# A fused attention and SwiGLU kernel: the RMSNorm of the first two batches taken out of the activations and put into the gate product, the output and the copies

## The chip, the cores and the metric

The kernel runs on one core of one Trainium2 chip. The metric is the device time of one execution in microseconds (us). Four executions of the kernel before gave 471.46 to 472.03 us, with a median of 471.5. The span of a profiled execution, from the first to the last instruction, is about 2 us shorter than its time (469.9 for 471.5).

In the profile, PE is the matmul engine (TensorE), DVE the vector engine, ACT the scalar engine (ScalarE), POOL the GpSimd engine. "L314" is a line of the kernel that was profiled. Line numbers move between kernels, so I compare groups by the names of their tiles.

## The reference

Eight batches, twelve heads, 448 tokens, head size 64. Attention has one more term in the denominator ("softmax off by one"). Its result becomes 3584 tokens of 768 features, which go through RMSNorm and a SwiGLU block (768 to 1536 to 768). Inputs and outputs are fp32; the kernel multiplies in bf16.

```python
scores = q @ k.T / sqrt(64)
m      = max(scores);  e = exp(scores - m)
x      = e / (sum(e) + exp(-m)) @ v          # -> 3584 x 768
xn     = x / sqrt(mean(x*x) + 1e-6) * rms_g  # RMSNorm, per token
g, val = xn @ w_gate, xn @ w_val             # 768 -> 1536
out    = (g * sigmoid(g) * val) @ w_out      # 1536 -> 768
```

Two facts of this algebra make the change possible. The factor 1/rms is one number per token, so it may be multiplied in after a product as well as before it. The factor rms_g is one number per feature, so it may sit in x or in the weights.

## The kernel before

PE follows one program order in which the feed-forward of a batch (24 "products" of 6 matmuls, gate and value in turn) is mixed with the attention of the next batch. DVE and ACT work in their own program orders: before 40.17 us of the trace DVE stood 1.68 us for a tanh. Batches 0 and 1 (`NPE = 2`) turn x on PE; the later batches turn it by DMA.

The normalization of x in batches 0 and 1, with 1/rms per token (`rinv`), then the turn of x on PE:

```python
def emit_scale(b, c):
    nc.vector.tensor_scalar(out=x_tiles[b][:, c, :], in0=x_tiles[b][:, c, :],
                            scalar1=xnt_tiles[b, "r"][:, c:c + 1], ...)
def emit_turn_x(b, c):
    if b < NPE:
        ps = ps_f.tile([128, KD, P], BF16, name="xnt_ps", tag="f")
        for dk in range(KD):
            nc.tensor.transpose(ps[:, dk, :], xn[:, c, dk * 128:(dk + 1) * 128], ...)
        # copied to xnt_sb by ACT or DVE
    else:
        nc.sync.dma_start_transpose(out=xnt[:, c, :, :], in_=xn[:, c, :])
```

A product and what follows it. `t_sb` is tanh(g/2), and (t_sb + 1) * g is twice g * sigmoid(g); the output's factor 0.5 takes the 2 back. I call the DVE instruction that makes `silu` the *second step*.

```python
def emit_A(b, m, part):
    ...
    for dk in range(KD):
        nc.tensor.matmul(ps[:, 0:S], lhsT=w[:, dk, m * 128:(m + 1) * 128], rhs=xnt_tiles[b][:, :, dk, :], ...)
    if part == 0:   # gate
        nc.scalar.activation(out=t, in_=ps[:, 0:S], func=AF.Tanh, scale=0.5)
        nc.vector.scalar_tensor_tensor(out=u, in0=t, scalar=1.0, in1=ps[:, 0:S], op0=ALU.add, op1=ALU.mult)
    else:           # value
        nc.vector.tensor_tensor(out=ht_tiles[...], in0=g_cur.pop((b, m)), in1=ps[:, 0:S], op=ALU.mult)
```

Between batch 0's attention and its feed-forward. `scale_w` multiplies rms_g into a piece of the weights; `warm` issues matmuls that only keep PE busy.

```python
emit_root(0)            # mean of squares, then POOL's power: rinv
scale_w(2, V); scale_w(1, A)
warm(14)
for c in range(C):
    emit_scale(0, c)
scale_w(1, V)
for c in range(C):
    emit_turn_x(0, c)
...                     # more scale_w
```

The softmax here doesn't subtract the row's maximum and nothing guards it: scores larger than these inputs give would overflow.

## Time and profile before

| | before |
|---|---|
| median of 4 executions | 471.5 us |
| profiled span, mean clock of PE | 469.9 us, 0.998 |
| PE busy | 456.2 us (97%) |
| DVE busy | 240.8 us (51%) |

The table of busy time in the profile page of the kernel before (share of the span, count of instructions):

```profile
PE 456.2 (97%) x4051; PEld 246.0 (52%) x4051; DVE 240.8 (51%) x621; ACT 249.4 (53%) x365; POOL 95.4 (20%) x109
```

The table of stretches of the kernel before. The rows are: the last attention of batch 0 to its first product, batch 0's feed-forward with batch 1's attention, batch 1's feed-forward with batch 2's attention, and the rest. The columns are the stretch and its length, the busy time and count of each engine, PE's granted clock, the DMA share and GB/s:

```profile
core 0: us, PE busy (x) PEld busy (x) DVE busy (x) ACT busy (x) POOL busy (x), PEclk, DMA share, GB/s
29.15:35.21 6.06, 5.23 (x56) 3.02 (x53) 4.99 (x19) 4.20 (x9) 1.15 (x1) 1.00 1.30 240
35.21:88.43 53.22, 48.46 (x533) 25.09 (x533) 39.34 (x94) 33.24 (x49) 23.67 (x27) 1.00 0.89 175
88.43:126.03 37.60, 37.60 (x343) 19.37 (x342) 21.78 (x53) 23.03 (x32) 9.40 (x9) 1.00 0.84 169
126.03:469.90 343.87, 339.48 (x2774) 184.20 (x2770) 156.50 (x402) 166.57 (x249) 43.71 (x42) 1.00 0.52 111
```

PE is full in batch 1's feed-forward (37.60 busy of 37.60 us). What can be won lies earlier. PE's timeline there (start, busy time, line, what was computed, and in brackets the idle time before it with what ended it):

```profile
29.03 3.19 PE L360 MATMUL warm_ps<-blank 128*128 128x512 bf16 x14
32.79 1.73 PE L280 MATMUL xnt_ps<-identity,x_sb 112*128 112x112 bf16 x24 [0.57 <-DVE x_sb L271]
...
35.21 1.30 PE L314 MATMUL g_ps<-xnt_sb,wg_bf 128*128 128x448 bf16 x6
```

The 3.19 us of warming matmuls are time in which PE has no real work, because x is still being normalized. This is the hole that the change aims at. PE's list of waits from 35 to 89 us (total, times, longest), its three largest, shows how little it waits for in batch 0's feed-forward:

```profile
PE g_ps L314 <- DVE ht_sb L325: 1.8, 1, 1.8
PE u_ps L240 <- DVE x_sb L244: 1.5, 3, 1.1
PE v_ps L314 <- DVE wv_bf L125: 0.7, 1, 0.7
```

### The profile page before, as it was taken

To read this page: it belongs to the slowest core of one execution; us is meant where nothing else is said; L and a number is where in the kernel's file an instruction comes from. 1 tells how busy PE (TensorE), PEld (TensorE's weight loads), DVE (VectorE), ACT (ScalarE), POOL (GpSimd) and SP (SyncE) were. 2 spreads that over 40 slices of the span, in tenths; PEclk is the share of its full clock that TensorE was granted. 3 is DMA by queue.
4 is the path that set the end of the run, shared out by engine and by line. 5 is a ranking of instruction groups with operands and counts; after the bars stand their busy time and mean duration, and the time that the engine had idled before them with its cause. 6 is when DMAs were issued, how large, how long until landed. Compare 5 with 4: busy or idle time off the path is not lost.

```text
span 469.9 us, 9847 instructions
## 1 busy us (share of the span) xinstructions
PE 456.2 (97%) x4051; PEld 246.0 (52%) x4051; DVE 240.8 (51%) x621; ACT 249.4 (53%) x365; POOL 95.4 (20%) x109
## 2 busy tenths in 40 slices
PE   8989997999999999999999999999999999999996
PEld 3554543554555555455465545545455555555563
DVE  4676698445632176645742265854743247555200
ACT  4987763655566565464546555555556652222221
POOL 7434454114012211322002211313000000000000
PEclk9999999999999999999999999999999999999999
DMA  8999974999079896495049988299015221100133
GB/s 130 223 224 200 212 178 101 213 220 207 1 157 206 214 203 146 85 214 115 0 108 202 227 188 161 45 183 174 14 36 126 69 68 22 38 1 0 36 100 102
DMA packets 86937, 60.48 MB, mean 129 GB/s; under 512 B 50678, under 2 KB 81980, under 8 KB 86892
## 3 DMA queue, kind: packets, MB, share of 16 engines
q1 hardware_dynamic: 73980, 43.60, 43.5%
q0 software_dynamic: 12912, 16.26, 18.7%
q8 instruction: 32, 0.52, 0.5%
q14 instruction: 13, 0.11, 0.1%
HBM read 47.19 MB, written 11.01 MB: 124 GB/s over the span
## 4 chain that ended last, share of the span: by engine, by line
PE 89%; DVE 4%; ACT 2%; DMA 1%; issue 1%; POOL 1%; ACTq 0%; POOLq 0%
PE o_ps L339 24%; PE v_ps L314 23%; PE g_ps L314 18%; PE u_ps L240 10%; PE s_ps L209 9%; PE s_ps L314 5%; DMA k_bf<-in_k_dram 1%; ACT p_sb_110 L214 1%; DVE x_sb L271 1%; PE qkt_ps L182 1%; DVE x_sb L244 1%; ACT p_sb_108 L214 1%; ACT t_sb L318 1%; DVE wv_bf L125 0%; DVE xsq L266 0%
## 5 line engine op out<-in xcount | busy, mean ns | idle before, releaser
L314 PE MATMUL v_ps<-xnt_sb,wv_bf 128*128 128x448 bf16 x576 | 125.1, 353 | 0.7 <-DVE wv_bf L125 0.7
L339 PE MATMUL o_ps<-wo_bf,ht_sb 128*128 128x384 bf16 x672 | 116.5, 326 | 0.0
L314 PE MATMUL g_ps<-xnt_sb,wg_bf 128*128 128x448 bf16 x444 | 96.4, 353 | 1.9 <-DVE ht_sb L325 1.8
L339 PEld LDWEIGHTS <-ht_sb 128*128 128x128 bf16 x672 | 62.6, 98 | 46.2 <-issue 7.8
L314 PEld LDWEIGHTS <-wg_bf 128*128 128x128 bf16 x576 | 52.2, 97 | 55.3 <-issue 12.3
L314 PEld LDWEIGHTS <-wv_bf 128*128 128x128 bf16 x576 | 52.4, 98 | 52.5 <-issue 8.2
L318 ACT ACTIVATE t_sb<-g_ps 128x448 f32<-128x448 f32 x74 | 40.3, 545 | 67.6 <-PE g_ps L314 67.6
L214 ACT ACTIVATE p_sb_108<-s_ps 112x896 bf16<-112x896 f32 x64 | 55.6, 915 | 14.9 <-PE s_ps L209 14.8
L214 ACT ACTIVATE p_sb_110<-s_ps 112x896 bf16<-112x896 f32 x64 | 55.9, 915 | 12.5 <-PE s_ps L209 12.5
L342 ACT ACTIVATE out_sb<-o_ps 128x384 f32<-128x384 f32 x56 | 27.5, 491 | 65.2 <-PE o_ps L339 55.8
L214 ACT ACTIVATE p_sb_109<-s_ps 112x896 bf16<-112x896 f32 x64 | 55.8, 918 | 10.2 <-PE s_ps L209 10.2
L243 DVE RECIPROCAL recip<-u_ps 112x4 f32<-112x4 f32 x96 | 17.1, 178 | 80.2 <-PE u_ps L240 80.1
L244 DVE TENSOR_TENSOR x_sb<-u_ps,recip 112x256 bf16<-112x256 f32 x96 | 40.7, 424 | 3.3
L158 POOL CAST q_bf<-q_f 112x1024 bf16<-112x1024 f32 x17 | 17.7, 1043 | 101.0 <-DMA q_f<-in_q_dram 75.7
L209 PE MATMUL s_ps<-qk_t 64*128 64x448 bf16 x272 | 37.5, 354 | 0.0
L297 POOL TENSOR_TENSOR rinv<-ms,neghalf 112x4 f32<-112x4 f32 x8 | 8.3, 1032 | 143.8 <-DVE ms L291 138.8
L266 DVE CUSTOM_DVE_ANT_0 xsq<-x_sb 112x256 bf16<-112x256 bf16 (+3 forms) x62 | 33.9, 547 | 1.6
L318 ACT ACTIVATE t_sb<-s_ps 128x448 f32<-128x448 f32 x22 | 12.0, 544 | 38.5 <-PE s_ps L314 33.3
L314 PE MATMUL s_ps<-xnt_sb,wg_bf 128*128 128x448 bf16 x132 | 28.6, 352 | 0.0
L240 PEld LDWEIGHTS <-p_sb_110 112*128 112x128 bf16 (+1 forms) x512 | 19.6, 97 | 7.8 <-DVE x_sb L244 1.4
L240 PEld LDWEIGHTS <-p_sb_109 112*128 112x128 bf16 (+1 forms) x512 | 19.9, 97 | 5.9 <-issue 1.2
L240 PEld LDWEIGHTS <-p_sb_108 112*128 112x128 bf16 (+1 forms) x512 | 19.3, 98 | 7.0 <-issue 2.7
(278 smaller groups left out, 382.7 us busy)
## 6 DMA issues: line engine op xcount, KB each, us to landing
q_f<-in_q_dram SPq DMA_DIRECT2D x15, 448.0 KB, 4.7
k_f<-in_k_dram SPq DMA_DIRECT2D x15, 448.0 KB, 6.0
v_f<-in_v_dram SPq DMA_DIRECT2D x15, 448.0 KB, 7.4
v_f<-in_v_dram POOLq DMA_DIRECT2D x9, 448.0 KB, 8.7
out_dram<-out_sb SPq DMA_DIRECT2D x7, 336.0 KB, 3.0
wg_bf<-in_moe_w_gate_dram POOLq DMA_DIRECT2D x2, 1152.0 KB, 16.3
wv_bf<-in_moe_w_val_dram POOLq DMA_DIRECT2D x2, 1152.0 KB, 14.5
wo_bf<-in_moe_w_out_dram POOLq DMA_DIRECT2D x3, 768.0 KB, 13.6
```

What stands on the lines that cost most here:

```text
L158: eng.tensor_copy(out=dst, in_=staged[n, i].rearrange("p h c d -> p c h d"))
L209: nc.tensor.matmul(s_ps[:, hh, 0:S], lhsT=k_t[r, k0:k0 + 128], rhs=qs[r], start=True, stop=True)
L214: nc.scalar.activation(out=p_v, in_=s_ps[0:P, :, 0:S], func=AF.Exp, scale=scale)
L240: nc.tensor.matmul(u_ps[:, qc, :], lhsT=p_sb[0:K, q0:q0 + 128], rhs=v_sb[0:K, c, h, :], start=(c == 0), stop=(c == C - 1))
L243: nc.vector.reciprocal(out=recip, in_=u_ps[0:P, :, D:E1])
L244: nc.vector.tensor_tensor(out=x_tiles[b][:, :, h * D:(h + 1) * D], in0=u_ps[0:P, :, 0:D], in1=recip.to_broadcast([P, C, D]), op=ALU.mult)
L266: nc.vector.tensor_tensor_reduce(out=xsq[:, 0:n], in0=x_c, in1=x_c, scale=1.0, scalar=0.0, op0=ALU.mult, op1=ALU.add, accum_out=acc)
L297: nc.gpsimd.tensor_tensor(out=rinv, in0=ms, in1=neghalf, op=ALU.pow)
L314: nc.tensor.matmul(ps[:, 0:S], lhsT=w[:, dk, m * 128:(m + 1) * 128], rhs=xnt_tiles[b][:, :, dk, :], start=(dk == 0), stop=(dk == KD - 1))
L318: nc.scalar.activation(out=t, in_=ps[:, 0:S], func=AF.Tanh, scale=0.5)
L339: nc.tensor.matmul(o_ps[:, 0:HN], lhsT=ht_tiles[b2][:, fk, c * 128:(c + 1) * 128], rhs=wo_bf[:, fk, n * HN:(n + 1) * HN], start=(fk == 0), ...
L342: nc.scalar.activation(out=o_sb[:, n * HN:(n + 1) * HN], in_=o_ps[:, 0:HN], func=AF.Copy, scale=0.5)
```

## The change

The intent: do not wait for 1/rms before the first products. x of batches 0 and 1 is turned raw, two heads (a "pair") at a time, as soon as attention has made it. rms_g goes into the copies of the turned pairs, so the weights need no scaling at first; the 24 scalings of the weights move to later, for batches 2 to 7. 1/rms is multiplied into the gate product (it must go in before tanh) and into the output, where it takes care of the value product. For the gate it is needed as a row along the free axis, the same on all partitions: a diagonal matrix is built by DVE and multiplied by ones on PE (the "spread"). For the output it is needed as 7 columns: eight tiny fp32 matmuls. The change also re-times what stands around it: batch 1's attention starts 3.5 units later in the schedule of batch 0's feed-forward (5.7 instead of 2.2, where a product is 1.13 units), and POOL's loads and casts move with it.

The core of the diff (cut at each "..."):

```diff
+    def emit_turn_pair(b, j, eng):
+        ps = ps_f.tile([128, C, P], BF16, name="xnt_ps", tag="f")
+        for c in range(C):
+            nc.tensor.transpose(ps[:, c, :], x_tiles[b][:, c, j * 128:(j + 1) * 128], ...)
+        # copied by ACT or DVE, times gain[:, j:j + 1]
+    def emit_diag(b):
+        nc.vector.tensor_tensor(out=diags[b]..., in0=identity..., in1=xnt_tiles[b, "r"]..., op=ALU.mult)
+    def emit_spread(b):
+        nc.tensor.matmul(ps, lhsT=ones, rhs=diags[b], start=True, stop=True)
+        nc.scalar.copy(out=rinv_b[b], in_=ps)
+    def emit_columns():
+        ...  # eight times
+                nc.tensor.matmul(ps[done:done + take, i:i + 1], lhsT=rinv_b[b][0:1, t:t + take],
+                                 rhs=ones[0:1, 0:1], start=True, stop=True)
+        nc.vector.tensor_scalar(out=rinv_c, in0=ps, scalar1=0.5, ...)
...
+                gate = ps[:, 0:S]
+                if b < NPE:
+                    gate = out_pool.tile(...)[:, 0:S]
+                    nc.vector.tensor_tensor(out=gate, in0=ps[:, 0:S], in1=rinv_b[b], op=ALU.mult)
+                nc.scalar.activation(out=t, in_=gate, func=AF.Tanh, scale=0.5)
+                nc.vector.scalar_tensor_tensor(out=u, in0=t, scalar=1.0, in1=gate, ...)
...
-                             func=AF.Copy, scale=0.5)
+                             scale=rinv_c[:, c:c + 1] if 2 * b2 < NPE else 0.5)
...
+    for j in range(NP):
+        ops.append((T1 + STEP * (j + 1) + 2.5 + (j == NP - 1), lambda j=j: emit_turn_pair(1, j, (A, V)[j % 2])))
+    for i in range(2 * KD):
+        ops.append((42.0 + 1.0 * i, lambda: scale_w(1, V)))
+        ops.append((55.0 + 1.9 * i, lambda: scale_w(1, V)))
...
     emit_AV(NP - 1, 1)
-    scale_w(1, A)
+    emit_A(0, 0, 0, 0, KD - 1, "s")      # three products, as far as pairs 0 to 4 go
+    emit_A(0, 0, 1, 0, KD - 1)
+    emit_turn_pair(0, NP - 1, A)
     emit_root(0)
-    scale_w(2, V)
-    warm(14)
-    ...                                  # emit_scale, emit_turn_x, scale_w
+    load_w(1)                            # a weight load issued by POOL
+    cast_qkv(NG, 2, G)                   # a cast by POOL
+    emit_A(0, 1, 0, 0, KD - 1, "s")
+    emit_A(0, 0, 0, KD - 1); emit_A(0, 0, 1, KD - 1); emit_A(0, 1, 0, KD - 1)
+    emit_diag(0)
+    emit_spread(0)
+    emit_A(0, 1, 1)
+    emit_T(NP)                           # q and k of batch 1's first pair turned
+    emit_A(0, 2, 0, bank="u")
```

## The prediction

> **What bounds the kernel.** TensorE (PE): busy 456.2 of 469.9 us (busy table), clock 0.998. The table of stretches shows no PE idle time from 88 to 420 us. What can be won lies earlier: the start of the feed-forward, and 4.7 us of PE idle from 51 to 82 us.
>
> **The aim.** PE's timeline from 29.0 to 35.2 us, between batch 0's last attention product and the first feed-forward matmul: 14 warming matmuls (3.2 us), 0.57 idle, 24 transposes of x (1.73), transposes of q/k (0.5). DVE's timeline shows why: squares, POOL's power, scalings, turn. Afterwards most of three products starts at once, on raw x.
>
> **Removed and moved.** Warm block, idle, turning of x: about 5.3 us of PE. In 51 to 82 us, 12 weight scalings on DVE (0.33 to 1.19 us each) and batch 1's scalings of x (three took 3.1 us); PE waited 0.74 us for a scaled weight and 1.76 + 0.36 us for DVE there (list of waits); these should go.
>
> **Added (estimates from the trace).**
> - The 1/rms chain now sits in PE's order. The pair's copy (0.5 us) stands before ScalarE's squares, then power 1.15, diagonal 0.6, [...]copy 0.5. PE should idle about 2 us before the spread, and 1.9 us more before batch 1's first q/k transposes, whose bank the first value product still holds. So most of the 5.3 us comes back: at 42 us at most 1 us ahead.
> - Pair copies in batch 0, where DVE is full: 0.45 us.
> - 24 gate multiplies on DVE, 0.54 us each like the other 448-column fp32 operations: 13 us. Worse, gate multiply, tanh and second step are consecutive on an in-order DVE. [...]the trace agrees (DVE idles 1.0 to 1.7 us for t_sb). So DVE stands 0.7 us per gate, and a gate/value pair holds it 2.3 us, where PE needs 2.27, or 3.15 with attention between.
> - Batch 1's feed-forward (88 to 126 us, PE full, DVE 22 of 38 us) gets 12 of these, plus 12 weight scalings (up to 1.2 us beside a POOL cast) in its second half. DVE then needs about 22 us where PE needs 17. Three banks and the next stage absorb perhaps 2 us; I expect 2 to 5 us of PE waiting.
> - [...]columns 0.5 us of PE.
>
> **Sum.** Start -0.5 (-3 to +1); batch 0's feed-forward -1.5 (-4 to +1); columns +0.5; batch 1's feed-forward +3 (0 to +6). From 150 us on nothing changes. That gives 473; as I may overstate DVE's standing, I predict **472.0 us, range 465.5 to 478.5**. Chances: faster by over 2% 0.03, within 2% 0.88, slower by over 2% 0.09.
>
> **What would show it.** PE timeline: no warm block at 29 us; 2 us idle before the fp32 spread; a second wait before batch 1's first q/k transposes. Without these the start gains 3 us. PE waits: scaled weights gone; new ones on DVE's products in batch 1's feed-forward. DVE timeline: gate multiply, gap of 0.7 us, second step; busy time up by 9 us.
>
> **What would make it wrong.** If free banks cover DVE's standing, PE stays full in batch 1's feed-forward and the result is 466 to 468. Value weights landing late (30.1 us before, just when needed) would add up to 1 us.

The sum came to -0.5 - 1.5 + 0.5 + 3 = +1.5 us on 471.5, which is the 473. The 0.5 us for the columns and the 2 us that banks absorb are estimates, without a trace behind them.

## The result, and the profile after

The changed kernel is correct and slower: a median of 490.95 us (four executions, 489.71 to 494.2) against 471.5. The ratio is 1.042, with a 95% interval of 1.037 to 1.0471. Ratios here are the mean time of one kernel's fast runs over that of the other's fast runs of the same rounds, so they are not quite the ratio of the medians that I quote. The profiled span grew from 469.9 to 488.9 us, by 19.0. This is far outside the predicted range.

Busy time in the profile page after, and the table of stretches. The rows are now: the first product to batch 1's first scores, just before the seventh product (46.28 us); to batch 1's first product; to the first output product; the rest. Two short stretches are put between:

```profile
PE 461.9 (94%) x4054; PEld 249.3 (51%) x4054; DVE 257.7 (53%) x649; ACT 248.8 (51%) x363; POOL 95.5 (20%) x109
```

```profile
core 0: us, PE busy (x) PEld busy (x) DVE busy (x) ACT busy (x) POOL busy (x), PEclk, DMA share, GB/s
30.59:46.28 15.69, 11.45 (x64) 5.19 (x61) 8.55 (x21) 3.01 (x8) 2.96 (x3) 0.78 1.19 218
37.00:38.00 1.00, 0.00 (x0) 0.00 (x0) 0.96 (x1) 0.00 (x0) 0.47 (x1) 0.50 1.15 209
46.28:98.93 52.65, 42.46 (x498) 22.92 (x499) 35.65 (x79) 31.88 (x47) 23.38 (x27) 1.00 0.78 163
98.93:144.16 45.23, 41.75 (x359) 21.72 (x357) 31.15 (x73) 21.13 (x30) 7.40 (x7) 0.96 0.51 107
127.00:129.00 2.00, 2.00 (x8) 0.59 (x5) 1.30 (x4) 1.48 (x3) 0.00 (x0) 0.50 0.00 0
144.16:488.90 344.74, 339.72 (x2768) 184.38 (x2767) 162.67 (x419) 169.79 (x251) 44.19 (x42) 1.00 0.52 110
```

PE is now idle for 10.2 us of batch 0's main stretch and for 3.5 us of batch 1's feed-forward, and its clock was halved twice, from 36.9 to 43.7 us and from 125.7 to 129.1. The starts of the products in the two timelines divide the 19.0 us:

| stretch | before | after | difference |
|---|---|---|---|
| up to the seventh product of batch 0 | 46.78 | 46.77 | 0.0, but see below |
| from there to batch 1's first product | 41.65 | 52.16 | +10.5 |
| from there to the first output product | 37.60 | 45.23 | +7.6 |
| from there to the end | 343.87 | 344.74 | +0.9 |

The first row is not as even as it looks. At its seventh product the kernel before had also done two turns of q and k, three groups of scores and two attention products of batch 1, which the changed kernel had not: 3.6 us of PE by the durations in the trace (0.5, 0.49 and 0.55 each). So of the +10.5 in the second row 3.6 is carried from the start, and 6.9 is lost in batch 0's feed-forward itself.

PE's timeline after:

```profile
30.59 1.11 PE L367 MATMUL s_ps<-xnt_sb,wg_bf 128*128 128x448 bf16 x5
...
38.11 1.83 PE L328 MATMUL r_ps<-t_sb,ones 112*128 112x448 f32 x2 [3.75 <-DVE t_sb L320]
39.73 2.45 PE L367 MATMUL v_ps<-xnt_sb,wv_bf 128*128 128x448 bf16 x6
42.11 0.58 PE L190 MATMUL qkt_ps<-identity,q_bf 112*64 112x112 bf16 x8
...
80.17 0.36 PE L217 MATMUL s_ps<-pair_t_111 64*128 64x448 bf16 x2 [1.11 <-ACT p_sb_115 L222]
...
85.97 0.37 PE L292 MATMUL xnt_ps<-identity,x_sb 112*128 112x112 bf16 x4 [1.88 <-DVE x_sb L252]
...
123.28 0.94 PE L343 MATMUL c_ps<-ones,rinv_b_102 1*128 1x1 f32 x7 [1.89 <-DVE x_sb L252]
...
124.97 1.79 PE L367 MATMUL g_ps<-xnt_sb,wg_bf 128*128 128x448 bf16 x6
...
127.55 2.04 PE L367 MATMUL v_ps<-xnt_sb,wv_bf 128*128 128x448 bf16 x6
```

The first product does start 4.6 us earlier (30.59 against 35.21). Then PE stands 3.75 us before the spread, and the work after it runs at half clock: the value product at 39.73 takes 2.45 us where a product takes 1.30. Half clock comes again behind the columns, from 125.7 us.

The wait before the spread ends with DVE's diagonal. The timelines of DVE and of POOL at that place, and of DVE in batch 0's feed-forward:

```profile
35.60 2.37 DVE L320 TENSOR_TENSOR t_sb<-identity,rinv 112x448 f32<-112x448 bf16 x1 [1.16 <-POOL rinv L309]
...
66.64 0.62 DVE L378 TENSOR_TENSOR out_sb<-g_ps,rinv_b_102 128x448 f32<-128x448 f32 x1 [1.27 <-PE g_ps L367]
67.96 0.63 DVE L382 SCALAR_TENSOR_TENSOR silu_1100<-t_sb,out_sb 128x448 bf16<-128x448 f32 x1 [0.70 <-ACT t_sb L380]
68.51 0.17 DVE L251 RECIPROCAL recip<-u_ps 112x4 f32<-112x4 f32 x1
68.72 0.42 DVE L252 TENSOR_TENSOR x_sb<-u_ps,recip 112x256 bf16<-112x256 f32 x1
69.06 0.61 DVE L387 TENSOR_TENSOR ht_sb<-silu_1100,v_ps 128x448 bf16<-128x448 bf16 x1
```

```profile
34.52 1.04 POOL L309 TENSOR_TENSOR rinv<-ms,neghalf 112x4 f32<-112x4 f32 x1 [6.98 <-DVE ms L307]
35.54 0.88 POOL L119 DMA_DIRECT2D wv_bf<-in_moe_w_val_dram  x1
36.42 1.06 POOL L166 CAST v_sb_117<-v_f 112x1024 bf16<-112x1024 f32 x1
```

The diagonal takes 2.37 us. At 66.64 the new chain is seen: gate multiply, 0.70 us in which DVE stands for tanh, second step, and only then the attention's division (`x_sb`, from `recip` at 68.51 us on; the `u_ps` that it reads was done at 67.09) and the value step (`ht_sb`), for which PE's next work waits. That DVE stands for tanh is not new. The kernel before had it too, without a multiply in front:

```profile
43.66 0.62 DVE L320 SCALAR_TENSOR_TENSOR silu_857<-t_sb,g_ps 128x448 bf16<-128x448 f32 x1 [1.80 <-ACT t_sb L318]
```

In batch 0's feed-forward such waits sum to 10.8 us before and 8.2 after. What is new is that DVE itself must first multiply, when it gets to it, before ACT can start tanh. ACT's timeline shows the same chain from the other side:

```profile
78.74 0.58 ACT L380 ACTIVATE t_sb<-out_sb 128x448 f32<-128x448 f32 x1 [2.65 <-DVE out_sb L378]
79.22 3.32 ACT L222 ACTIVATE p_sb_115<-s_ps 112x896 bf16<-112x896 f32 x4
```

ACT stood 2.65 us for the gate multiply. The exponentials that attention needs (`p_sb`) queue behind that tanh: they start at 79.22 us, though PE had ended their first scores by 77.32. PE waited 1.11 us for them at 80.17. PE's list of waits of the whole execution after, its five largest:

```profile
PE xnt_ps L292 <- DVE x_sb L252: 5.6, 8, 1.9
PE r_ps L328 <- DVE t_sb L320: 4.6, 2, 3.8
PE s_ps L217 <- ACT p_sb_115 L222: 2.9, 6, 1.1
PE c_ps L343 <- DVE x_sb L252: 1.9, 1, 1.9
PE s_ps L217 <- DVE pair_t_109 L193: 1.6, 1, 1.6
```

The wait for scaled weights is gone. In its place are waits for x of the pair to be turned, for the diagonal, for exponentials, and for the bank of the columns.

### The profile page after: what moved, and what is told of

It is laid out like the page before. It is cut to its first block, busy times and chain, and to the rows that moved or that the text cites. A ratio compares the mean times of both kernels' runs of the same rounds, so it can differ in the third digit from the quotient of the medians.

```text
span 488.9 us, 9880 instructions
## 1 busy us (share of the span) xinstructions
PE 461.9 (94%) x4054; PEld 249.3 (51%) x4054; DVE 257.7 (53%) x649; ACT 248.8 (51%) x363; POOL 95.5 (20%) x109
## 4 chain that ended last, share of the span: by engine, by line
PE 78%; issue 7%; DMA 4%; POOL 4%; DVE 4%; ACT 2%; POOLq 0%; ACTq 0%; DVEq 0%
PE o_ps L405 22%; PE v_ps L367 19%; PE g_ps L367 14%; PE u_ps L248 8%; PE s_ps L217 7%; PE s_ps L367 5%; DMA q_f<-in_q_dram 1%; DMA v_f<-in_v_dram 1%; DMA k_bf<-in_k_dram 1%; ACT p_sb_115 L222 1%; DVE x_sb L252 1%; POOL v_sb_117 L166 1%; ACT t_sb L380 1%; DVE out_sb L378 1%; DVE xsq L274 1%
## 5 line engine op out<-in xcount | busy, mean ns | idle before, releaser
L367 PE MATMUL v_ps<-xnt_sb,wv_bf 128*128 128x448 bf16 x576 | 127.0, 357 | 0.0
L367 PE MATMUL g_ps<-xnt_sb,wg_bf 128*128 128x448 bf16 x432 | 94.6, 355 | 1.2 <-DVE ht_sb L387 1.2
L380 ACT ACTIVATE t_sb<-g_ps 128x448 f32<-128x448 f32 x50 | 27.2, 544 | 50.1 <-PE g_ps L367 50.1
L408 ACT ACTIVATE out_sb<-o_ps 128x384 f32<-128x384 f32 x42 | 20.6, 491 | 50.1 <-PE o_ps L405 45.9
L217 PE MATMUL s_ps<-qk_t 64*128 64x448 bf16 x272 | 38.6, 357 | 1.8 <-ACT p_sb_115 L222 1.3
L380 ACT ACTIVATE t_sb<-out_sb 128x448 f32<-128x448 f32 x24 | 13.8, 577 | 43.7 <-DVE out_sb L378 43.7
L367 PE MATMUL s_ps<-xnt_sb,wg_bf 128*128 128x448 bf16 x144 | 31.3, 352 | 0.0
L248 PEld LDWEIGHTS <-p_sb_115 112*128 112x128 bf16 (+1 forms) x512 | 19.8, 97 | 6.4 <-DVE qk_t L173 0.9
L248 PEld LDWEIGHTS <-p_sb_113 112*128 112x128 bf16 (+1 forms) x512 | 19.4, 98 | 7.0 <-issue 3.0
```

The source lines that it names most:

```text
L217: nc.tensor.matmul(s_ps[:, hh, 0:S], lhsT=k_t[r, k0:k0 + 128], rhs=qs[r], start=True, stop=True)
L248: nc.tensor.matmul(u_ps[:, qc, :], lhsT=p_sb[0:K, q0:q0 + 128], rhs=v_sb[0:K, c, h, :], start=(c == 0), stop=(c == C - 1))
L380: nc.scalar.activation(out=t, in_=gate, func=AF.Tanh, scale=0.5)
L408: nc.scalar.activation(out=o_sb[:, n * HN:(n + 1) * HN], in_=o_ps[:, 0:HN], func=AF.Copy, scale=rinv_c[:, c:c + 1] if 2 * b2 < NPE else 0.5)
```

## The experiments

My theory after reading the two traces: most of the loss comes from the 24 gate multiplies, which lengthen a chain through two engines that work in order (DVE stood 0.70 us and ACT 2.65 us above, with work behind them), mainly in batch 0's feed-forward where attention shares those engines. The rivals: (1) the start, that is, the long diagonal and the halved clock behind it; (2) the 24 scalings of weights that now fall into batch 1's feed-forward, as the prediction feared; (3) the places of the new small work in PE's order, namely the turns of batch 1's pairs and the columns. Each expectation below names its own pair of theories; "A" and "B" are not the same from one to the next. "Changed" is the kernel after the change with its 490.95 us. The kernel before gave medians between 471.5 and 472.63. Each profile is one execution; the times come from all.

### POOL's load and cast moved behind the diagonal

```diff
     emit_root(0)
-    load_w(1)
-    cast_qkv(NG, 2, G)
...
     emit_diag(0)
+    nc.gpsimd.tensor_copy(out=pool_gate, in_=diags[0][0:1, 0:1])   # POOL waits for the diagonal
+    load_w(1)
+    cast_qkv(NG, 2, G)
```

> The changed kernel, but POOL's weight load and value cast come after the first diagonal (a one-element POOL copy of the diagonal makes it wait). In the changed kernel the diagonal took 2.37 us and ended 0.49 us after POOL's cast ended (37.48 to 37.97). Theory A [...]: the diagonal takes about 0.6 us, PE's idle time before the first spread falls from 3.75 to about 2.0 us, the clock no longer falls there, and the kernel gets 4 to 5 us faster than the changed one (486 us). Theory B (the diagonal is slow by itself, from its broadcast operands): it still takes about 2.4 us and the time stays at 491 us.

Measured: 491.74 us (490.64 to 492.01), ratio 1.040. The diagonal fell from 2.37 to 0.62 us and PE's idle time before the spread from 3.75 to 2.01. Still the clock halved at about 36.6 us (0.50 until 40.0), and the time did not move. In the profiled execution this kernel was 2.4 us ahead of the changed one at the ninth product (50.81 against 53.24) and still at the nineteenth (79.35 against 81.79). Then its clock fell once more, from 84 to 91 us, where the changed kernel's had not, and at batch 1's first product nothing was left (99.07 against 98.93). So the shorter diagonal is no gain.

The slow diagonal is also not in every execution. It took 2.35 to 2.37 us in seven of the eight profiles of kernels that leave POOL's cast where the change put it, but 0.63 us in the eighth, that of the later turns (below), though POOL's load and cast start at the same distance from it there as in the changed kernel:

```profile
35.30 0.63 DVE L320 TENSOR_TENSOR t_sb<-identity,rinv 112x448 f32<-112x448 bf16 x1 [1.16 <-POOL rinv L309]
...
36.12 1.06 POOL L166 CAST v_sb<-v_f 112x1024 bf16<-112x1024 f32 x1
```

With the cast moved it took 0.62 or 0.63 us in all four profiles. So the cast next to it is tied to the slow diagonal, but does not always bring it. How often the executions without a profile had it is not known.

### POOL's cast alone moved

The same edit, with the load left where it was and only the cast behind the diagonal.

> The changed kernel with only POOL's value cast moved behind the first diagonal; its weight load is still issued while the diagonal runs. Theory A (issuing the load holds DVE's two-operand multiply up as well): the diagonal takes about 1.3 us, ending about 0.5 us after the issue ends. Theory B (only the cast[...] does): the diagonal takes 0.62 us. The time is not expected to differ from 491 us by more than 1 us in either case.

Measured: 492.71 us in one execution (its state is unknown; before gave 471.69). DVE's and POOL's timelines of this kernel:

```profile
35.07 0.63 DVE L321 TENSOR_TENSOR t_sb<-identity,rinv 112x448 f32<-112x448 bf16 x1 [1.16 <-POOL rinv L310]
```

```profile
35.00 0.87 POOL L120 DMA_DIRECT2D wv_bf<-in_moe_w_val_dram  x1
...
36.01 1.04 POOL L167 CAST v_sb<-v_f 112x1024 bf16<-112x1024 f32 x1
```

The issue of the load runs beside the diagonal from 35.07 to 35.70 and costs it nothing here. This fits the cast as the cause of the 1.75 us, but it is one execution, and one of eight with the cast in place was as fast.

### Warming matmuls in the wait before the spread

```diff
     emit_diag(0)
+    fill = ps_u.tile([128, 512], FP32, name="fill_ps", tag="u")
+    for _ in range(15):
+        nc.tensor.matmul(fill, lhsT=blank[:, 0:128], rhs=blank, start=True, stop=True)
     emit_spread(0)
```

> The changed kernel with 15 warming matmuls (about 3.2 us) in PE's wait before the first spread; the wait itself stays as long. Theory A (the slow matmuls after that wait come from the clock that fell in it): the stretches from 38 to 45 us show clock 1.00 instead of 0.50 to 0.57, the first value product after the spread takes 1.3 instead of 2.45 us, and the kernel is about 2.5 us faster than the changed one (488.5 us). Theory B (those matmuls are slow for another reason, such as the fp32 product ahead of them, and the clock only goes along): they stay slow and the time stays at 491 us.

Measured: 491.82 us (491.25 to 493.7), ratio 1.0417: no gain. PE's timeline of this kernel:

```profile
38.48 0.99 PE L328 MATMUL r_ps<-t_sb,ones 112*128 112x448 f32 x2 [0.51 <-DVE t_sb L320]
39.30 1.30 PE L367 MATMUL v_ps<-xnt_sb,wv_bf 128*128 128x448 bf16 x6
...
45.80 0.55 PE L217 MATMUL s_ps<-pair_t 64*128 64x448 bf16 x3 [1.77 <-DVE pair_t L193]
```

The clock stayed at 1.00 there, the spread took 0.82 us (38.48 to 39.30) and the value product 1.30 instead of 2.45. PE then waited 1.77 us at the next scores, for DVE's copy of the turned q and k (`pair_t`), which stands behind the gate chains. So the halved clock at the start is real, but DVE paces this place: what PE saves it waits for, and at the seventh product only 0.5 us are left (46.28 against 46.77). Later in this profile the clock fell from 81 to 85 us, where it had not in the changed kernel. Rival (1) is out as the main cause.

### The columns by DMA instead of on PE

The tiny matmuls became 14 small transfers straight from `rinv`, with DVE's factor 0.5 applied later.

```diff
-                nc.tensor.matmul(ps[done:done + take, i:i + 1], lhsT=rinv_b[b][0:1, t:t + take], ...)
+                nc.sync.dma_start(out=rinv_c[done:done + take, i:i + 1],
+                                  in_=xnt_tiles[b, "r"][p0:p0 + take, c:c + 1])
```

> The changed kernel, but the column form of 1/rms for the output is copied by small DMAs from the root itself instead of 16 one-column fp32 matmuls on PE. Theory A (wait for the bank 1.9 us, the tiny matmuls 1.7 us, and a clock that falls to half for about 4 us after them): 5 to 5.5 us faster than the changed kernel (485.5 us), clock 1.00 throughout 118 to 133 us. Theory B (the wait is only DVE's backlog, which PE meets at the next bank anyway): only the 1.7 us of tiny matmuls come back, perhaps 1.8 us of clock: 487.5 to 489 us.

Measured: 488.29 us (486.87 to 493.41), ratio 1.0351. The steps from one product to the next around the columns went from 5.39, 2.58 and 2.38 us to 1.65, 1.72 and 1.64, that is, 5.3 us less. Only about 2.7 us of this are in the time. In the profile 1.5 us came back a few products later as a wait of PE for exponentials, and the clock fell at another place (86 to 93 us), where it had not in the changed kernel.

### The gate multiply left out (a wrong result)

```diff
-                if b < NPE:
+                if False:
                     gate = out_pool.tile(...)
```

> The changed kernel without the 24 gate multiplies on DVE (result wrong on purpose; everything else, the spread too, stays). Theory A (gate multiply, tanh and second step in a row hold DVE, and ScalarE's exps queue behind tanh, so that both feed-forward stages of batches 0 and 1 stretch): 6 to 9 us faster than the changed kernel (482 to 485 us), and PE's waits for DVE's x and for ScalarE's exps between 46 and 99 us mostly vanish. Theory B (DVE's standing is hidden by the free banks, and the loss is all in the 1/rms chain, columns and clock): under 2 us faster.

Measured: 479.55 us (478.56 to 480.29), ratio 1.0145. The result was wrong (relative error 0.494). The multiplies are worth 11.4 us of the 19.5. From the seventh product to batch 1's first this kernel takes 45.52 us (46.52 to 92.04), against 52.16 in the changed one and 41.65 before. The excess over the kernel before is 3.9, and 3.6 of it is the attention work carried from the start: the 6.9 us lost in batch 0's feed-forward are gone. Batch 1's feed-forward takes 42.23 us instead of 45.23. PE's only wait left there was 1.2 us for the bank of the columns, and in batch 0's there was none for exponentials.

### The kernel before, with 24 multiplies by ones

The same instruction in the other kernel, where nothing else is new:

```diff
+            gate = ps[:, 0:S]
+            if b < NPE:
+                gate = out_pool.tile([128, DM], FP32, name="out_sb")[:, 0:S]
+                nc.vector.tensor_tensor(out=gate, in0=ps[:, 0:S], in1=ones, op=ALU.mult)
-            nc.scalar.activation(out=t, in_=ps[:, 0:S], func=AF.Tanh, scale=0.5)
+            nc.scalar.activation(out=t, in_=gate, func=AF.Tanh, scale=0.5)
```

> The kernel before, with one thing added: the gate of batches 0 and 1 is multiplied on DVE by a tile of ones into the same buffer, ahead of tanh (24 multiplies, result right). Leaving the multiplies out of the changed kernel gave 12 us. Theory A (the multiplies cost by themselves, through DVE and ScalarE's order): 6 to 12 us slower than the kernel before (478 to 484 us). Theory B (they cost that much only together with the other waits and clock falls of the changed kernel): 1 to 4 us slower (473 to 476 us), clock 1.00 throughout.

Measured: 482.99 us (482.24 to 484.5) against 471.76, ratio 1.0239: +11.2 us. In the profiled execution 8.9 of it were there by batch 1's first product (97.33 against 88.43) and only 1.1 came in batch 1's feed-forward (38.70 us against 37.60). The clock was halved once in it, from 89.0 to 92.4 us, so up to 1.7 of the 8.9 (half of 3.4) may be the clock. PE's list of waits of this kernel from 35 to 98 us, its three largest:

```profile
PE u_ps L242 <- DVE x_sb L246: 4.3, 4, 2.3
PE v_ps L316 <- DVE wv_bf L127: 1.9, 2, 1.2
PE s_ps L211 <- DVE pair_t L187: 1.9, 3, 1.0
```

PE waits where attention needs DVE: a bank that the division has not freed, a weight not yet scaled, a turned pair not yet copied. Both directions agree on 11 us, and this is the theory's main support.

### The second step issued one product later

In the changed kernel, the second step of a gate is put into DVE's order just before the value step that needs it, so that other DVE work may come between multiply and second step.

```diff
-                u = ...; nc.vector.scalar_tensor_tensor(out=u, in0=t, scalar=1.0, in1=gate, ...)
-                g_cur[b, m] = u
+                g_cur[b, m] = (t, gate)
             else:
+                g_cur[b, m] = second(*g_cur[b, m])    # the same instruction, here
```

> The changed kernel, but in batches 0 and 1 the second step of the gate is given to DVE only with the value product, so that DVE need not stand between gate multiply and second step. Theory A (what costs is DVE standing about 0.7 us at each of 24 gates): 3 to 6 us faster than the changed kernel (485 to 488 us), and DVE's waits of 0.7 us for tanh are gone. Theory B (what costs is the multiply's own 0.54 us and that ScalarE's exps queue behind a tanh that now waits for DVE): less than 1.5 us faster.

Measured: 484.73 us (484.66 to 486.57), ratio 1.0271, 6.2 us less than the changed kernel. Nothing of the work is gone, so this much is the order of DVE's queue and not the busy time of the multiplies. DVE's waits for tanh, which were expected to go, fell from 16.4 us over 24 gates to about 7. PE's waits for exponentials did not shrink (4.7 us from 30 to 150 us, 3.6 in the changed kernel): tanh still waits for the multiply, and the exponentials stand behind it.

### The same in the kernel before with multiplies by ones

> The kernel before with the 24 multiplies by ones (which alone made it 11 us slower), and the second step of the gate given to DVE with the value product. Theory A (DVE standing for tanh between multiply and second step is the larger part): at most 5 us slower than the kernel before (up to 476.5 us). Theory B (the multiply's own 0.54 us and the later tanh are the larger part): 6 to 10 us slower (477.5 to 481.5 us).

Measured: 476.64 us (475.94 to 477.05) against 472.38, ratio 1.009. Of the +11.2 us, 4.3 are left. About 7.0 of the 11.2 were the order of the queue.

### The multiply in place in PSUM

```diff
-                    gate = out_pool.tile([128, DM], FP32, name="out_sb")[:, 0:S]
-                    nc.vector.tensor_tensor(out=gate, in0=ps[:, 0:S], in1=rinv_b[b], op=ALU.mult)
+                    nc.vector.tensor_tensor(out=gate, in0=ps[:, 0:S], in1=rinv_b[b], op=ALU.mult)  # gate is ps
```

> The changed kernel, but the gate multiply writes back into its own PSUM bank, so that the second step again reads one SBUF operand and one PSUM operand, as in the kernel before. In the changed kernel three second steps took 0.82 to 1.67 us instead of 0.62, beside POOL casts (1.7 us in excess together); in the kernel before none did. Theory A [...]: no second step above 0.7 us, and the kernel 1 to 2 us faster than the changed one (489 to 490 us). Theory B (the operand's place does not matter): they stay, 491 us. Against both stands that the bank is now held until the second step.

Measured: 490.69 us (488.25 to 492.13), ratio 1.0386. Some second steps in the changed kernel took long (1.67, 0.82 and 1.10 us instead of 0.63), and here none took over 0.7, but the time stayed. So those slow second steps do not set the time. (The edit also holds the bank longer, which may cost something of its own.)

### All scalings of the weights moved out of batch 1's feed-forward

```diff
-        ops.append((42.0 + 1.0 * i, lambda: scale_w(1, V)))
-        ops.append((55.0 + 1.9 * i, lambda: scale_w(1, V)))
+        ops.append((55.0 + 1.9 * i, lambda: scale_w(2, V)))    # all in the output stage
```

> The changed kernel with all 24 weight scalings in the output stage of batches 0 and 1 (12 of them stood in the second half of batch 1's feed-forward). From the third last gate product of batch 1 on to the second output product the changed kernel lost about 2.8 us against the one before. Theory A (the prediction's: DVE cannot take the scalings there beside the gate multiplies): those 2.8 us come back, 488 us. Theory B: the loss there is the one-column products' and the clock's alone, and the time stays within 1 us of 491.

Measured: 490.56 us (489.33 to 491.86), ratio 1.0396. No change beyond the spread of the runs. In the profile batch 1's feed-forward took 44.1 us instead of 45.2, so rival (2), one of the prediction's two costs in that stage, is worth about 1 us there at most and is not seen in the time.

### Batch 1's pairs turned later

The turns of batch 1's pairs on PE were moved 1.2 units later in the schedule (about one product), because PE waited for `x_sb` before three of them (0.92, 0.93 and 1.88 us).

```diff
-        ops.append((T1 + STEP * (j + 1) + 2.5 + (j == NP - 1), ...
+        ops.append((T1 + STEP * (j + 1) + 3.7 + (j == NP - 1), ...
```

> The changed kernel with batch 1's transposes of x 1.2 schedule units later, so that a product stands between them and the attention product whose result they turn. In the changed kernel PE waited 0.92 + 0.93 + 1.88 us for x there. Theory A (these waits are avoidable by order alone): they vanish and the kernel is 2 to 4 us faster (487 to 489 us). Theory B (DVE is behind, and PE meets the same backlog at the next bank): less than 1 us.

Measured: 487.05 us (484.43 to 488.46), ratio 1.0314, 3.9 us less. The waits before the turns are gone from PE's list. Rival (3) holds for a part: turns were placed before DVE could have the pair ready. The profile alone would mislead: its seventh product came 2.9 us earlier than in the changed kernel (43.88 against 46.77), mainly because its diagonal happened to take 0.63 us and its clock did not fall there. From there to batch 1's first product it gained 3.5 us (48.64 against 52.16), which the turns can explain, and at the columns it lost 2.1.

### The four together, and the four with filled waits

The POOL order, the later second step, the later turns and the columns by DMA in one kernel.

> The changed kernel with four of the single edits together: POOL's load and cast after the first diagonal, the second step of the gate given with the value product, batch 1's transposes of x later, and the columns by DMA. Apart they gave 0, 6, 4 and 3 us. Theory A (they remove different waits, and clock falls are what hid the first): the sum and a bit more, 476 to 479 us. Theory B (they share one backlog on DVE): 481 to 484 us.

Measured: 478.59 us (478.21 to 479.0) against 472.63, ratio 1.0135. This takes 12.4 us off the changed kernel. The single effects sum to 12.8 (6.2 + 3.9 + 2.7 + 0). It remains 6.0 us slower than before, and the 24 multiplies with a deferred second step alone account for 4.3 of that in the kernel before.

Then warming matmuls were put into its waits in batch 0's attention and before the spread:

```diff
+    warm(1)     # four times in batch 0's attention
+    for _ in range(9): nc.tensor.matmul(fill, ...)    # before the spread
```

> The same, with four warming matmuls put back into batch 0's attention and nine into PE's wait before the first spread. Theory A [...]: no fall below 1.00 before 50 us, and 1.5 to 3 us faster than the combined kernel. Theory B (the falls cost nothing, as PE would wait anyway): the same time as the combined kernel within 1 us.

Measured: 478.75 us (477.97 to 478.95), ratio 1.0135. The clock did not fall before 50 us, and the time was the same: PE waited 1.77 us for `pair_t` instead. At the start a full clock buys nothing while DVE is behind.

### The kernel before without its warming matmuls

To see what the clock costs where DVE is not behind, 17 warming matmuls (14 before x is turned, 3 during batch 0's attention) were left out.

```diff
-        (2, 0): [lambda: warm(1), lambda: set_v(1)],
+        (2, 0): [lambda: set_v(1)],
...
-    warm(14)
```

> The kernel before without 17 of its warming matmuls: the three in batch 0's attention that the change replaced and the 14 before the turn of x. Nothing waits for them, so no wait gets longer. Theory A (in the light stretches PE's clock falls to half without them): falls to 0.50 in at least one stretch of several us before 45 us, and 2 to 4 us slower (474 to 476 us). Theory B (the clock does not depend on them): 471 to 472 us, clock 1.00.

Measured: 473.84 us (472.68 to 474.22), ratio 1.003 (1.0005 to 1.0055). The clock was halved from 31 to 38 us. PE's timeline of this kernel:

```profile
32.69 2.42 PE L280 MATMUL xnt_ps<-identity,x_sb 112*128 112x112 bf16 x24 [3.59 <-DVE x_sb L271]
...
35.94 2.30 PE L314 MATMUL g_ps<-xnt_sb,wg_bf 128*128 128x448 bf16 x6
```

The turns took 2.42 instead of 1.73 us and the first product 2.30 instead of 1.30, and 1.5 us of it showed in the time. So the 17 warming matmuls of the kernel before were worth about 1.5 us (0.2 to 2.6 by the interval), which the prediction had not counted against their removal.

### Only the half of the change that moves rms_g

The kernel before, with rms_g in the copies of pairs and the weights scaled in the first output stage as in the change, but with 1/rms still multiplied into x, and so no gate multiply, no spread and no columns.

```diff
-    scale_w(1, A)
     emit_root(0)
-    scale_w(2, V); scale_w(1, A)
     warm(14)
     for c in range(C): emit_scale(0, c)
-    for c in range(C): emit_turn_x(0, c)
+    for j in range(NP): emit_turn_pair(0, j, (A, V)[j % 2])
```

> The kernel before with only the second half of the change: rms_g goes into the copies of the turned x, pair by pair, and the weights are scaled in the first output stage; 1/rms stays on x, so there is no gate multiply, no spread and no columns. Theory A (what was good in the change is to take the 24 weight scalings away from batch 0's feed-forward, where PE waited 0.74 us for a weight and several times for DVE): 2 to 4 us faster than the kernel before (467.5 to 469.5 us). Theory B (there is nothing to win, the turn by pairs costs as much): 471 to 473 us.

Measured: 476.35 us (475.62 to 476.56), ratio 1.0084. It was 1.2 us ahead at the twentieth product (76.18 against 77.41), then PE waited 0.89, 0.89 and 0.63 us at batch 1's turns, and the clock fell from 81.7 to 88.5 us. So the turns of batch 1 were moved 1.7 units later and put closer together:

```diff
-        ops.append((22.2 + 0.75 * j, lambda j=j: emit_turn_pair(1, j, ...)))
+        ops.append((23.9 + 0.56 * j, lambda j=j: emit_turn_pair(1, j, ...)))
```

> The kernel of e12 (gain in the copies, weights scaled in the first output stage, 1/rms still on x), with the pair transposes of batch 1 later, after DVE's four scalings of its x, for which PE waited there and after which its clock fell. Up to the 20th product e12 was 1.2 us ahead of the kernel before. Theory A (only that wait and the clock fall made e12 slower): no clock fall between 80 and 90 us, and 1 to 2.5 us faster than the kernel before (469 to 470.5 us). Theory B (turning by pairs costs DVE and ScalarE more there whatever its place): 472 us or more.

Measured in five rounds: 471.46 us (470.68 to 473.79) against 472.38, ratio 0.9991 (0.9962 to 1.002): the same. Its profile had no clock fall before its last 2 us, and batch 1 started at 87.46 us instead of 88.43. It is not shown to beat the kernel before. The half that moves rms_g costs nothing if its turns are well placed; the half that moves 1/rms, with the re-timing that came with it, carries the loss.

## Why the prediction was wrong, point by point

**What was right.** PE's timeline after has no warming block and starts products earlier. The wait for scaled weights is gone. DVE does the gate multiply, stands 0.64 to 0.70 us, and does the second step. The multiply takes 0.62 us (0.54 estimated). DVE's busy time rose by 16.9 us, where 9 were expected. The spread took 0.82 us at full clock (38.48 to 39.30, with warming matmuls), or 4.3 times the 0.19 of a bf16 matmul of the same 448 columns (six start within 1.13 us). The range and the chances were wrong: slower by over 2% was given 9%.

**"Batch 0's feed-forward -1.5" is the step that failed most.** It measured +6.9. The prediction counted DVE's work that goes away (scalings of weights and of x) against the work that comes (pair copies, multiplies) and compared sums of a gate and value pair, 2.3 us on DVE with 2.27 to 3.15 on PE. A sum cannot see an order. Gate multiply, tanh and second step are three steps on two in-order queues. Whatever stands behind them waits: on DVE the division of attention, the copy of turned q and k and the value step, and on ACT the exponentials. PE needs those to go on, and then the next gate product comes late. The prediction took DVE as in order and named its idle time for `t_sb`; the trace shows the same of ACT (it stood 2.65 us for a multiply with exponentials behind it). The mistake was to count it for DVE alone, as 0.7 us per gate in a sum. Taking the multiplies away gave 11.4 us and brought this stage's 6.9 down to 0.3, adding them to the other kernel cost 11.2, and moving only the second step gave back 6.2 and 7.0. How the rest divides between ACT's exponentials and the multiplies' own time on DVE no run separates.

**"Batch 1's feed-forward +3 (0 to +6)" was too small, and mostly for other reasons than given.** It measured +7.6. The scalings of weights, named beside the multiplies as the cause, were not seen in the time when they were moved. About 5.3 of the 7.6 came in three products around the columns: a wait of 1.9 us, 1.7 us of tiny matmuls, and about 1.8 us of half clock behind them. PE's waits for exponentials and for `ht_sb` gave another 1.6. The multiplies, which I expected to hurt most here, cost 1.1 us in this stage in the kernel before, and leaving them out of the changed kernel gave 3.0.

**"Columns 0.5 us of PE" and "columns +0.5".** The term, an estimate without a trace behind it, was mis-sized. The tiny matmuls took 1.7 us (123.28 to 124.97), and the bank they need had to be freed by DVE first (1.9 us).

**"Start -0.5".** By the count above the start was 3.6 us worse. "Diagonal 0.6" was right by itself (0.62) but 2.37 us in most profiles with POOL's cast right behind it, where the change puts it. The "2 us" of idle before the spread were 3.75 for that reason. The "1.9 us more before batch 1's first q/k transposes" did not come there; a wait came at the next scores instead, for DVE's copy: 0.49 us in the changed kernel, at half clock until then, and 1.77 where the clock was kept up. The experiments show that repairing the diagonal or the clock at this place gains nothing while DVE is behind. But the 3.6 stays when the multiplies are left out, so it is not theirs; whether the wait for 1/rms or the re-timed attention makes it is not tested.

**The clock was left out.** The kernel before had no fall in its profile until its last 2 us; the changed kernel's had two, of 6.8 and 3.4 us at half clock. The prediction removed the warming block and counted only its 3.2 us as gain. By the experiment without them, the block and three more warming matmuls are worth 1.5 us in the kernel before. How much of the 19.5 the clock makes up is bounded rather than measured: by estimate these falls could cost at most 5.1 us in the profiled execution (half of 10.2, the sum of 6.8 and 3.4), and the two experiments that removed falls at the start gained nothing.

**What stays open.** The four repairs together leave 6.0 us, of which 4.3 is also seen with the multiplies alone; the other 1.7 is not assigned. Of the 8 us that are left without the multiplies, the profile puts 3.9 in batch 0's feed-forward (3.6 of them carried from the start) and 4.6 in batch 1's, where the columns stand. The clock falls come at different places from execution to execution, also where the code is the same: two profiles (the gate multiply left out, the second step later) had one near 15 us, in code that they share with the changed kernel, and their first product came at 31.98 and 32.46 us instead of 30.59. This blurs the effect of single edits, and the stages above are those of one execution each. Why the POOL order moved no time without a profile is not known.

## What to carry to other kernels

When an elementwise step is moved from an input to a product, follow the new chain through each in-order queue and list what stands behind it; sums of busy time per stage, even with room in them, do not show the loss, and issuing the last step of the chain one product later won half of it back (6.2 of 11.4 us here, 7.0 of 11.2 in the other kernel). Moving a wait earlier does not remove it (PE stood 3.75 us before the spread). A hole in the matmul engine's work can cost twice, once as idle time and once as a lower clock (after a hole of 2.01 us the clock fell to 0.50 in three of four profiles), but where another engine paced the place, a full clock gained nothing (491.82 us with warming matmuls before the spread, 490.95 without). Read more than one profile before giving a cause to one slow instruction: the same diagonal took 0.63 or 2.37 us. Try the independent halves of a change singly: here the half that moved rms_g was free, once its turns were well placed, and the half that moved 1/rms carried the loss.

## What the runs show of the clock, the diagonal and the small matmuls

- The granted clock was 1.00 or 0.50. In the changed kernel it was 0.50 from 36.9 to 43.7 us and from 125.7 to 129.1; every fall that was read from end to end in a profile lasted 3.4 or 6.8 us. The clock fell after a single gap of 2.01 us (POOL's work moved, 34.1 to 36.1 us). It did so in three of the four profiles that have this gap, and not in the fourth (later turns, 34.07 to 36.08 us). It also fell in batch 0's attention where the longest wait was 0.81 us (second step deferred, 15.6 to 19.1 us). What share of idle time brings a fall, and why the same gap brings one or none, is not shown.
- The diagonal took 2.35 to 2.37 us in seven of eight profiles with the cast behind it and 0.63 us in the eighth, and 0.63 us beside the issue of a load alone (one profile). In the changed kernel the trace records the diagonal's start at 35.60 us and the cast's at 36.42, when a diagonal of 0.63 us would have been over (35.60 + 0.63); it ended 0.49 us after the cast. In the eighth profile the recorded starts lie the same way (35.30 and 36.12 us), and it took 0.63. So the recorded starts do not tell when the cast lengthens the diagonal, and no run shows by what it does so.
- Eight small fp32 matmuls with one column (16 instructions, 192 to 266 ns each at full clock) took 1.7 us with their weight loads (123.28 to 124.97 us).
